# Attention block of a three-stage kernel: where TensorE issues the weighted-value products of a half

## The chip, the cores and the metric

One NeuronCore of a Trainium2 chip runs the whole program. The metric is device time in microseconds (us) of one execution. The engines have these names in the rows: PE is TensorE's matmul and PEld its weight load, DVE is VectorE, ACT is ScalarE, POOL is GpSimd, SP is the engine whose queue issues the DMAs.

## The reference

Three stages follow each other. The change lies in the first, a clustered attention over 2 batches, 8 heads, 768 tokens and 64 values a head:

```
mask = q_assign[:, :, :, None] == k_assign[:, :, None, :]      # nearest centroid of query and of key
scores = scale * np.matmul(q, k.transpose(0, 1, 3, 2))
scores = np.where(mask, scores, -1000000000.0)
scores = scores - np.max(scores, axis=-1, keepdims=True)
attn = np.exp(scores)
attn = attn / (np.sum(attn, axis=-1, keepdims=True) + 1e-09)
return np.matmul(attn, v)
```

Its output, 1536 tokens of 512 values, goes through a feed-forward block with a rational activation (512 to 2048 to 512) and one with a gated SiLU (512 to 1536 to 512).

## The kernel before

The heads are taken in eight pairs (two heads of a batch). The 768 queries of a pair are cut into two halves of 384, a half into three query blocks of 128, and for each query block there is one step per head: six steps a half, twelve a pair, 96 in all (the list `order`, PER = 6). `n` counts the steps.

A step consists of four parts. `scores` computes 128 queries by 768 keys on TensorE into a PSUM tile s_ps, of which there are two: two matmuls at L376 and two more at L380, which add the remainders and the mask. `maximum` (VectorE, L389) reduces the rows. `exponentials` (ScalarE, L397) writes p and the row sums. `transposes` turns p with six TensorE transposes (L435), three into each of two PSUM tiles t_ps, of which there are three, and two copies to SBUF (L440 on ScalarE; the second copy is VectorE's, L438, in the steps of `dve_evac`). The transposes are issued two steps behind the scores (LAG = 2): TensorE's order is scores(n), transposes(n-2), scores(n+1), transposes(n-1).

Once all six steps of a half are transposed, `weighted` multiplies them by the values: six key blocks (kb = 0 to 5) accumulate in the single PSUM bank o_ps, each with one matmul for each of the two heads (L446). The trace shows every such matmul as two records, so a half has 24. `normalised` (VectorE, L454) multiplies o_ps by the reciprocals of the row sums, which came back by DMA (`spread` with its small transpose r_ps at L412, `bring_back`), and `split_x` (GpSimd, L466 and L467) writes the two parts that the next stage reads.

The main loop runs over units of two steps (n0 and n0 + 1). Three units make a half, so n0 % 6 is 0, 2 or 4. The key blocks of a half are put into the list `pv` at the end of the unit with remainder 0; each later unit takes two off at its end. The order on each engine is the order in which the program issues; nothing reorders it.

`background(n, engine)` issues other work along with the steps: the similarities of the next pair's queries and keys with the centroids (`sims`, L305, TensorE), their cluster masks (VectorE), the split of the next pair's queries and keys (GpSimd), and the unpacking of nine early weight blocks (L82 on ScalarE, L91 and L95 on VectorE). After the loop, `tail` issues the products of the last half in two parts between the first matmuls of the next stage (h_ps, L695).

Of the kernel before, what the change touches and what calls it, by code (L numbers as in the profile page):

```python
# [20 lines left out]
def tile_kernel(ctx, tc, q_t, k_t, q_s, k_s, v_l, cent, w_in, w_out, a_co, b_co, w_gate, w_val, w_o2, out):  # L21
# [5 lines left out]
    NB = S // P  # L27
# [96 lines left out]
    n0, n1 = 2 * GROUP1[0], 2 * GROUP1[1]  # L124
# [41 lines left out]
    PER = 2 * HB  # L166
# [45 lines left out]
    def keep_warm(n, to, x=None):  # L212
        for _ in range(n):
            for j in range(HB):
                nc.tensor.transpose(to[:, j, :], ident if x is None else x[:, 0:P], ident)  # L215
# [154 lines left out]
    def scores(b, hp, half, i, e):  # L370
        t = heads[b, 2 * hp + e]
        s_ps = ps_s.tile([P, S], F32, tag="s", name="s_ps")
        q0 = half * HALF + i * P
        qs = slice(q0, q0 + P)
        for lo, hi in CUT:
            nc.tensor.matmul(s_ps[:, lo:hi], t["q1"][:, qs], t["k1"][:, lo:hi], start=True, stop=False)  # L376
        if (b, hp, half, i, e) == order[0]:
            keep_warm(6, fill, oh[0])
        for lo, hi in CUT:
            nc.tensor.matmul(s_ps[:, lo:hi], t["q2"][0:KM, qs], t["k2"][0:KM, lo:hi], start=False, stop=True)  # L380
        if (i, e) == (0, 0):
            st = live["st", b, hp, half] = st_p.tile([P, 3, PER], F32, tag="st", name="st")
            nc.vector.memset(st[:, 2, :], 1e-9)
        live["s", b, hp, half, i, e] = s_ps

    def maximum(b, hp, half, i, e):
        st = live["st", b, hp, half]
        k = e * HB + i
        nc.vector.tensor_reduce(  # L389
            out=st[:, 0, k:k + 1], in_=live["s", b, hp, half, i, e], axis=AX.X, op=ALU.max, negate=True  # L390
        )

    def exponentials(b, hp, half, i, e):
        st = live["st", b, hp, half]
        k = e * HB + i
        p = live["p", b, hp, half, i, e] = p_p.tile([P, S], F32, tag="p", name="p")
        nc.scalar.activation(  # L397
            out=p, in_=live.pop(("s", b, hp, half, i, e)), func=AF.Exp, bias=st[:, 0, k:k + 1],
            accum_out=st[:, 1, k:k + 1],
        )  # L400

    def reciprocals(b, hp, half):
        st = live["st", b, hp, half]
        nc.vector.tensor_reduce(
            out=st[:, 0, :], in_=st[:, 1:3, :].rearrange("p a k -> p k a"), axis=AX.X, op=ALU.add
        )
        nc.vector.reciprocal(out=st[:, 0, :], in_=st[:, 0, :])

    def spread(b, hp, half):
        st = live.pop(("st", b, hp, half))  # L410
        r_ps = t_tile("r_ps")[0:PER, 0, :]
        nc.tensor.transpose(r_ps, st[:, 0, :], ident)  # L412
        rs = rs_p.tile([PER, P], F32, tag="rs", name="rs")
        nc.scalar.copy(out=rs, in_=r_ps)
        rd = tc.dram_tile([2, HALF], F32, name="rd")
        nc.sync.dma_start(out=rd.rearrange("e (i p) -> (e i) p", p=P), in_=rs)
        live["rd", b, hp, half] = rd

    def bring_back(b, hp, half):
        rd = live.pop(("rd", b, hp, half))  # L420
        rb = live["rb", b, hp, half] = rb_p.tile([P, HALF], F32, tag="rb", name="rb")
        for e in range(2):
            nc.sync.dma_start(out=rb[e * D:(e + 1) * D, :], in_=rd[e:e + 1, :].to_broadcast([D, HALF]))

    def transposes(b, hp, half, i, e, on_dve):
        p = live.pop(("p", b, hp, half, i, e))
        if i == 0:
            live["pt", b, hp, half, e] = pt_p.tile([P, NB, HALF], F32, tag="pt", name="pt")
        pt = live["pt", b, hp, half, e]
        qc = slice(i * P, (i + 1) * P)  # L430
        for g in range(2):
            t_ps = t_tile("t_ps")
            for j in range(HB):
                kb = g * HB + j
                nc.tensor.transpose(t_ps[:, j, :], p[:, kb * P:(kb + 1) * P], ident)  # L435
            ks = slice(g * HB, (g + 1) * HB)
            if g == 1 and on_dve:
                nc.vector.tensor_copy(out=pt[:, ks, qc], in_=t_ps)  # L438
            else:
                nc.scalar.copy(out=pt[:, ks, qc], in_=t_ps)  # L440

    def weighted(b, hp, half, kb):
        if kb == 0:
            live["o", b, hp, half] = ps_v.tile([P, HALF], F32, tag="o", name="o_ps")
        for e in range(2):
            nc.tensor.matmul(  # L446
                live["o", b, hp, half][e * D:(e + 1) * D, :], heads[b, 2 * hp + e]["v"][:, kb, :],
                live["pt", b, hp, half, e][:, kb, :], start=(kb == 0), stop=(kb == NB - 1),
                tile_position=(0, e * D),
            )  # L450

    def normalised(b, hp, half):
        x = live["x", b, hp, half] = x_p.tile([P, HALF], F32, tag="x", name="x")
        nc.vector.tensor_tensor(  # L454
            out=x, in0=live.pop(("o", b, hp, half)), in1=live.pop(("rb", b, hp, half)), op=ALU.mult
        )

    def split_x(b, hp, half):
        x = live.pop(("x", b, hp, half))
        done = 0  # L460
        while done < HALF:
            t, o = divmod(b * S + half * HALF + done, T)
            n = min(HALF - done, T - o)
            hi = x_hl[t][:, 0, hp, o:o + n]
            src = x[:, done:done + n]
            nc.gpsimd.tensor_scalar(out=hi, in0=src, scalar1=1.0, scalar2=0.0, op0=ALU.mult, op1=ALU.add)  # L466
            nc.gpsimd.tensor_tensor(out=x_hl[t][:, 1, hp, o:o + n], in0=src, in1=r32(hi), op=ALU.subtract)  # L467
            done += n
# [54 lines left out]
    def q_rows(t, half):  # L523
        nc.scalar.activation(
            out=t["q2"][D:D + 32, cols[half]], in_=t["t3"][32 * half:32 * half + 32, :],
            func=AF.Identity, scale=MASKED, bias=msk[32 * half:32 * half + 32, 1:2],
        )
# [13 lines left out]
    pv = []  # L541
# [48 lines left out]
                    load_qk(b, 2 * hp + 1)  # L590

    LAG = 2
    def next_weighted():
        if pv:
            step = pv.pop(0)
            weighted(*step)
            if step[3] == NB - 1:
                return step[:3]


    for n0 in range(0, len(order) + LAG, 2):
        for n in (n0, n0 + 1):
            if n < len(order):
                scores(*order[n])
                maximum(*order[n])
            if n == 1:
                keep_warm(3, fill)
            if n >= LAG:
                transposes(*order[n - LAG], n % (2 * PER) in dve_evac)
            if n < len(order):  # L610
                exponentials(*order[n])
            if n == 1:
                q_rows(h1, 1)
                for t in (h0, h1):
                    del t["t3"]
            if n % PER == 0 and n:
                reciprocals(*order[n - 1][:3])
            if n % PER == RS and n > PER:
                spread(*order[n - RS - 1][:3])
            elif n == len(order) + 1:  # L620
                spread(*order[-1][:3])
            if n % PER == BB and n > PER:
                bring_back(*order[n - BB - 1][:3])
            for engine in ("dma", "pe", "dve", "pool", "act"):
                background(n, engine)
        finished = next_weighted()
        finished = next_weighted() or finished
        if finished:
            normalised(*finished)
            split_x(*finished)  # L630
        if n >= LAG and (n - LAG) % PER == PER - 1:
            pv.extend([order[n - LAG][:3] + (kb,) for kb in range(NB)])
    bring_back(*order[-1][:3])
# [12 lines left out]
    with ExitStack() as mctx:  # L646
# [292 lines left out]
        for n in range(NS):  # L939
# [20 lines left out]
            if pipe:  # L960
                _, reciprocal, quotient, remainder = pipe.pop()
# [139 lines left out]
        asked = set()  # L1101
        LAG = {"act": 1.7, "dve": 1.7, "pool": 3.5, "dma": 5.5, "set": 0.0}

# [104 lines left out]
        _, reciprocal, quotient, remainder = pipe.pop()  # L1208
        mm, _ = project(*seq[NS - 3])
# [12 lines left out]
        mm, _ = project(*seq[NS - 2])  # L1222
# [199 lines left out]
```

## Time and profile before

| what | us |
|---|---|
| median of three runs | 780.5 (780.27 to 780.78) |
| span of the profiled execution, first to last instruction | 779.4 |
| median less span | 1.1 |
| TensorE matmul busy | 773.3 |
| VectorE, ScalarE, GpSimd busy | 594.4, 510.9, 457.4 |

The profiled execution's own time is recorded as its span; the median of the timed runs stands 1.1 us above it. A busy time is the sum of an engine's instructions without their overlaps. Ends of matmuls are modelled, so a busy TensorE is not TensorE at its peak.

### The profile page before, as it was taken

What the parts mean: (1) busy time and instruction counts of PE and PEld (TensorE: products, weight loads), DVE (VectorE), ACT (ScalarE), POOL (GpSimd) and SP (SyncE); (2) the same over time, 40 slices, a digit from 0 to 9 for tenths busy, and PEclk for the clock granted to TensorE, in tenths of its full rate; (3) what the DMA queues carried; (4) which work ended last, traced back from release to release, by engine and by line L of the source; (5) the groups of instructions that cost most, each with busy time, mean ns of one, the idle gap of its engine ahead of it and who ended that gap; (6) DMA issues with size and microseconds to landing.
All of it is one profiled execution on the core that took longest, in us unless ns stands there. A gap on an engine that the chain in (4) does not pass through costs nothing.

```text
span 779.4 us, 11585 instructions
## 1 busy us (share of the span) xinstructions
PE 773.3 (99%) x4119; PEld 637.7 (82%) x4119; DVE 594.4 (76%) x894; ACT 510.9 (66%) x984; POOL 457.4 (59%) x429
## 2 busy tenths in 40 slices
PE   8999999999999999999999999999999999999998
PEld 7666666666767888888888888999999999999997
DVE  7778787778659999989999999997565655675454
ACT  8777777777776788787777768646645545454331
POOL 6476797678334676767777688764354544534410
PEclk9999999999999999999999999999999999999999
DMA  7266436533322211211211111013222112120013
GB/s 224 76 203 205 153 99 202 178 115 114 98 79 78 81 56 66 70 55 56 81 55 53 56 33 49 27 55 100 90 82 81 55 55 82 55 81 28 1 41 122
DMA packets 27209, 67.94 MB, mean 87 GB/s; under 512 B 4464, under 2 KB 10832, under 8 KB 27152
## 3 DMA queue, kind: packets, MB, share of 16 engines
q1 hardware_dynamic: 27152, 67.21, 26.3%
q8 instruction: 32, 0.52, 0.3%
q14 instruction: 25, 0.20, 0.1%
HBM read 59.48 MB, written 3.19 MB: 80 GB/s over the span
## 4 chain that ended last, share of the span: by engine, by line
PE 98%; DVE 1%; SPq 1%; DMA 0%; ACT 0%; issue 0%; POOL 0%; POOLq 0%
PE c_ps L1012 23%; PE h_ps L695 17%; PE acc L751 17%; PE acc L1069 13%; PE o_ps L446 8%; PE t_ps L435 8%; PE s_ps L376 5%; PE s_ps L380 4%; PE w_ps L215 1%; PE sim L305 1%; SPq L366 1%; DMA k<-t 0%; DVE st L389 0%; PE r_ps L412 0%; PE acc L1368 0%
## 5 line engine op out<-in xcount | busy, mean ns | idle before, releaser
L1012 PE MATMUL c_ps<-r,wb 128*128 128x384 f32 x648 | 125.3, 336 | 0.0
L1012 PEld LDWEIGHTS c_ps<-r,wb 128*128 128x128 f32 x648 | 115.4, 188 | 6.0
L389 DVE TENSOR_REDUCE st<-s_ps 128x1 f32<-128x768 f32 x96 | 91.5, 953 | 31.3 <-PE s_ps L380 30.5
L397 ACT ACTIVATE p<-s_ps,st 128x768 f32<-128x768 f32 x96 | 87.7, 913 | 13.6 <-DVE st L389 13.3
L712 POOL TENSOR_TENSOR tmp<-tmp 128x512 f32<-128x512 f32 x46 | 67.9, 1475 | 48.1 <-ACT tmp L711 47.7
L440 ACT COPY pt<-t_ps 128x384 f32<-128x384 f32 x160 | 70.0, 482 | 37.8 <-PE t_ps L435 37.5
L1020 ACT COPY tmp<-c_ps 128x384 f32<-128x384 f32 x60 | 28.8, 480 | 87.3 <-PE c_ps L1012 87.3
L1091 POOL TENSOR_TENSOR part<-tmp,part 128x512 f32<-128x512 f32 x18 | 23.3, 1297 | 101.0 <-ACT tmp L1090 101.0
L435 PE MATMUL t_ps<-ident,p 128*128 128x128 f32 x576 | 78.7, 272 | 0.0
L446 PE MATMUL o_ps<-pt,v 128*64 128x384 f32 x384 | 72.3, 499 | 0.0
L435 PEld LDWEIGHTS t_ps<-ident,p 128*128 128x128 f32 x576 | 66.8, 141 | 4.7 <-issue 0.6
L735 POOL TENSOR_TENSOR g<-td,tmp 128x512 fp32r<-128x512 f32 x45 | 58.5, 1300 | 18.0 <-DVE td L730 18.0
L751 PE MATMUL acc<-g,r 128*128 128x512 f32 x288 | 69.0, 389 | 0.0
L1023 DVE TENSOR_TENSOR tmp<-tmp,c_ps 128x384 f32<-128x384 f32 x40 | 22.2, 555 | 58.9 <-ACT tmp L1020 45.1
L1012 PE MATMUL c_ps<-r,xw 128*128 128x384 f32 x336 | 65.4, 337 | 0.0
L751 PEld LDWEIGHTS acc<-g,r 128*128 128x128 f32 x288 | 54.0, 188 | 11.2
L1012 PEld LDWEIGHTS c_ps<-r,xw 128*128 128x128 f32 x336 | 60.0, 188 | 3.7
L695 PE MATMUL h_ps<-r 128*128 128x512 f32 x252 | 60.8, 391 | 0.0
L1069 PE MATMUL acc<-wb,g 128*128 128x512 f32 x216 | 59.4, 394 | 0.0
L376 PE MATMUL s_ps<-k,q 128*128 128x512 f32 x192 | 58.4, 385 | 0.2 <-ACT p L397 0.2
L695 PEld LDWEIGHTS h_ps<-r 128*128 128x128 f32 x252 | 47.1, 188 | 11.5 <-issue 1.8
L376 PEld LDWEIGHTS s_ps<-k,q 128*128 128x128 f32 x192 | 28.8, 189 | 31.7 <-ACT pt L440 18.0
(169 smaller groups left out, 1774.3 us busy)
## 6 DMA issues: line engine op xcount, KB each, us to landing
raw<-w_in_dram SPq DMA_DIRECT2D x16, 512.0 KB
raw<-w_out_dram SPq DMA_DIRECT2D x16, 512.0 KB
raw<-w_val_dram SPq DMA_DIRECT2D x12, 512.0 KB
raw<-w_gate_dram SPq DMA_DIRECT2D x12, 512.0 KB
raw<-w_o_dram SPq DMA_DIRECT2D x12, 512.0 KB
xa<-q_t_dram SPq DMA_DIRECT2D x14, 384.0 KB
xa<-k_t_dram SPq DMA_DIRECT2D x14, 384.0 KB
sq<-q_s_dram SPq DMA_DIRECT2D x8, 384.0 KB
```

The source lines that it names most:

```text
L376: nc.tensor.matmul(s_ps[:, lo:hi], t["q1"][:, qs], t["k1"][:, lo:hi], start=True, stop=False)
L389: nc.vector.tensor_reduce(out=st[:, 0, k:k + 1], in_=live["s", b, hp, half, i, e], axis=AX.X, op=ALU.max, negate=True)
L397: nc.scalar.activation(out=p, in_=live.pop(("s", b, hp, half, i, e)), func=AF.Exp, bias=st[:, 0, k:k + 1], accum_out=st[:, 1, k:k + 1],)
L435: nc.tensor.transpose(t_ps[:, j, :], p[:, kb * P:(kb + 1) * P], ident)
L440: nc.scalar.copy(out=pt[:, ks, qc], in_=t_ps)
L446: nc.tensor.matmul(live["o", b, hp, half][e * D:(e + 1) * D, :], heads[b, 2 * hp + e]["v"][:, kb, :], live["pt", b, hp, half, e][:, kb, :] ...
L695: nc.tensor.matmul(h_ps, w[:, wi, cs], x[:, xi, cc, :], start=(n == 0), stop=(n == 3 * NCC - 1))
L712: spread.tensor_tensor(out=tq, in0=tq, in1=tr, op=ALU.add)
L735: eng.tensor_tensor(out=g[:, 1, :], in0=td, in1=tr, op=ALU.mult)
L751: nc.tensor.matmul(acc[c], w[:, wi, cs], g[:, gi, :], start=(first and m == 0), stop=(last and m == 2))
L1012: nc.tensor.matmul(live2[key], set_of[f][:, wi, a, cs], x[xi][:, kc, :], start=(first and n == 0), stop=(n == last), skip_group_check=True,)
L1069: nc.tensor.matmul(acc2[j, c], g[:, gi, c * P:(c + 1) * P], w[:, wi, :], start=(f % 2 == 0 and m == 0), stop=(f % 2 == 1 and m == 2),)
```

## The change

The key blocks of a half are taken off the list in another rhythm. The unit with remainder 2, the first behind the one that filled the list, issues all six; the units with remainders 4 and 0 issue none. `normalised` and `split_x` stay at the end of the unit with remainder 0, which now takes the finished half from the list `done_pv`. The tail is unchanged.

```
     LAG = 2
+    BURST = {2: 6, 4: 0, 0: 0}
+    done_pv = []
     def next_weighted():
-        if pv:
-            step = pv.pop(0)
-            weighted(*step)
-            if step[3] == NB - 1:
-                return step[:3]
+        step = pv.pop(0)
+        weighted(*step)
+        if step[3] == NB - 1:
+            done_pv.append(step[:3])
...
-        finished = next_weighted()
-        finished = next_weighted() or finished
-        if finished:
+        for _ in range(min(BURST[n0 % PER], len(pv))):
+            next_weighted()
+        if n0 % PER == 0 and done_pv:
+            finished = done_pv.pop()
             normalised(*finished)
             split_x(*finished)
```

## Rows read from the trace of the kernel before

**Rows 1.** The page: the span, and the clock granted to TensorE in tenths by slice.

```profile
span 779.4 us, 11585 instructions
...
PEclk9999999999999999999999999999999999999999
```

**Rows 2.** Busy times by stretch: start:end, length, busy by engine (instructions), clock, DMA.

```profile
43.65:56.83 13.18, 13.18 (x88) 9.27 (x89) 10.41 (x18) 10.11 (x26) 12.54 (x16) 1.00 0.55 173
56.83:71.00 14.17, 14.17 (x96) 9.46 (x97) 10.60 (x18) 10.13 (x25) 6.91 (x10) 1.00 0.60 197
```

**Rows 3.** The chain of waits, 140 to 190 us: start, duration, engine, tile, line, records.

```profile
146.27 0.78 PE sim L305 x8
...
157.44 1.44 PE o_ps L446 x8
158.88 0.55 PE s_ps L376 x2
...
160.44 0.35 PE s_ps L376 x2
...
161.80 1.44 PE o_ps L446 x8
...
164.80 0.11 PE r_ps L412
```

**Rows 4.** The chain of waits, 217 to 240 us, the end of the stage.

```profile
220.02 1.44 PE o_ps L446 x8
...
228.97 2.95 PE h_ps L695 x12
231.91 2.09 PE o_ps L446 x12
```

**Rows 5.** TensorE's timeline, 200 to 224 us: scores behind a run of products.

```profile
203.72 0.62 PE L376 MATMUL s_ps<-k,q 128*128 128x512 f32 x2
```

**Rows 6.** ScalarE's timeline, 200 to 214 us; in brackets idle time before it.

```profile
200.70 0.86 ACT L440 COPY pt<-t_ps 128x384 f32<-128x384 f32 x2 [0.71 <-PE t_ps L435]
201.45 0.92 ACT L397 ACTIVATE p<-s_ps,st 128x768 f32<-128x768 f32 x1
...
202.34 0.69 ACT L82 ACTIVATE raw<-raw 128x512 f32<-128x512 f32 x1
202.90 0.87 ACT L440 COPY pt<-t_ps 128x384 f32<-128x384 f32 x2
...
205.78 0.90 ACT L397 ACTIVATE p<-s_ps,st 128x768 f32<-128x768 f32 x1 [0.24 <-DVE st L389]
```

**Rows 7.** VectorE's timeline, 200 to 214 us.

```profile
203.84 0.56 DVE L454 TENSOR_TENSOR x<-o_ps,rb 128x384 f32<-128x384 f32 x1 [0.30 <-PE o_ps L446]
204.73 0.96 DVE L389 TENSOR_REDUCE st<-s_ps 128x1 f32<-128x768 f32 x1 [0.34 <-PE s_ps L380]
205.61 0.55 DVE L438 COPY pt<-t_ps 128x384 f32<-128x384 f32 x1
206.07 0.98 DVE L95 SCALAR_TENSOR_TENSOR c<-raw,c 128x512 uint32<-128x512 uint32 x1
206.98 0.94 DVE L389 TENSOR_REDUCE st<-s_ps 128x1 f32<-128x768 f32 x1
```

**Rows 8.** TensorE's timeline, 19.6 to 29.95 us: steps with no products between.

```profile
20.22 0.59 PE L376 MATMUL s_ps<-k,q 128*128 128x512 f32 x2
...
21.98 0.62 PE L376 MATMUL s_ps<-k,q 128*128 128x512 f32 x2 [0.15 <-ACT p L397]
...
23.62 0.62 PE L376 MATMUL s_ps<-k,q 128*128 128x512 f32 x2
...
28.47 1.51 PE L446 MATMUL o_ps<-pt,v 128*64 128x384 f32 x8
```

**Rows 9.** ScalarE's timeline, the same stretch.

```profile
22.54 0.94 ACT L397 ACTIVATE p<-s_ps,st 128x768 f32<-128x768 f32 x1
```

**Rows 10.** TensorE's timeline, 36 to 45 us: a wait for a DMA.

```profile
37.93 0.58 PE L380 MATMUL s_ps<-k,q 80*128 80x512 f32 x2 [0.71 <-DMA k<-t]
```

## The prediction

> **What bounds the kernel now.** I read the page first, for the engine that fills the span and for its clock: the granted clock of TensorE is full in all 40 slices [rows 1], so nothing here is to be won or lost by the clock unless TensorE falls idle for long. Then I read the busy times by stretch, over a half of the attention stage without similarities and one with [rows 2]. TensorE is busy in every microsecond of both, 13.18 of 13.18 us and 14.17 of 14.17 us, while ScalarE has 10.11 and 10.13 us of work in them, VectorE 10.41 and 10.60 us. So TensorE sets the pace with some 3 us to spare on the other two, and what matters is its own order. The chain of waits gives this order [rows 3]: one step (scores, then six transposes) takes 160.44 to 161.80 = 1.36 us, the eight product records of a unit 1.44 us, and the step behind them 158.88 to 160.44 = 1.56 us. The reader is to see that the run of products costs 0.20 us more than its own 1.44 us, paid by the scores behind it.
>
> Next comes the price of a product inside a run. Eight records take 1.44 us [rows 3], twelve in the tail 2.09 us [rows 4]; so each further record costs (2.09 - 1.44)/4 = 0.163 us and the beginning of a run 1.44 - 8 x 0.163 = 0.14 us. Every entry into the products thus costs 0.14 + 0.20 = **0.34 us** beside the products.
>
> Last I read the other engines' pace where no products stand between the steps. The kernel before has such a stretch: before the first half is transposed there are no products, and from the scores at 21.98 us to the first products at 28.47 us four steps run alone [rows 8]. They take 6.49 us, 1.62 us each, where TensorE needs 1.36. ScalarE explains it: two copies 200.70 to 201.45 and an exponential with its read of the sum 201.45 to 202.34 make 0.75 + 0.89 = **1.64 us** a step [rows 6]. The score tile has two buffers, and scores wait for the exponentials two steps earlier: the exponentials at 22.54 us release the scores at 23.62 us, 1.08 us later [rows 8, 9].
>
> **The change part by part.** *What is removed and moved.* Per half, 24 records stand in one run behind the steps of remainder 2 and 3 instead of three runs of eight. The count of instructions is the same, and the moved ones issue no DMA; no queue but TensorE's has another order. Normalisation and split stay where they were on VectorE and GpSimd. TensorE by itself saves two entries a half, 2 x 0.34 = 0.68 us. The run takes 24 x 0.163 + 0.14 = 4.04 us.
>
> *Waits of the run itself.* The last transposed scores that it reads were copied a unit earlier, and its one accumulator bank must be free of the half before: normalisation (0.56 us [rows 7]) follows the maximum of remainder 1, and the run stands two steps later, at least 2.7 us by 1.36 us a step. I cost this at nothing; if that cover went, up to 0.56 us would be added to each of 15 runs, 8 us.
>
> *What is late next.* Behind the run wait the scores and transposes on TensorE, and for them VectorE's maxima and ScalarE's exponentials and copies. In its 4.04 us ScalarE can do only the backlog that the buffers hold and then idles; afterwards six steps come with no products between them, and ScalarE needs 1.64 us for each against TensorE's 1.36. I lay one half out from the moment the run ends (0), by rows.
> The scores start at 0; VectorE's maximum starts 1.01 us later (203.72 to 204.73) and the exponential 1.05 us after that, so at 2.06 [rows 5 to 7]. ScalarE has only the step's two copies before it (the transposes end at 1.56, the last copy some 0.4 behind them), and from here it goes without a gap: the next three exponentials come at 3.70, 5.34, 6.98. Scores of steps 3 to 6 need those of steps 1 to 4 plus 1.08: 3.14, 4.78, 6.42, 8.06, where TensorE alone would want some 2.7, 4.1, 5.5, 6.9. The last step ends 1.56 us after its start, as from 21.98 + 3 x 1.64 = 26.90 to 28.47 us [rows 8]: the next run starts at 9.62. TensorE alone needs 6 x 1.36 + 0.20 + 0.11 (the reciprocals' transpose [rows 3]) = 8.47. So 1.15 us of stall stand against 0.68 saved. The period becomes 9.62 + 4.04 = 13.66 us against 13.18: **+0.48 us**, in six halves of this kind = +2.88.
>
> The halves with similarities (0.78 us on TensorE [rows 3]) give the others that time. There VectorE copies half the tiles of the first two steps and shifts bits: maximum at 1.01, copy 1.89, shift 2.35, next maximum 3.26 (pitches 0.88, 0.46, 0.91 [rows 7]); so the exponentials stand at 2.06, 4.31, 5.95, 7.59, the last scores at 8.67, the next run at 10.23. The period is 14.27 against 14.17, +0.10, five times = +0.50.
>
> Four places differ. (a) The first half: the scores that waited 0.71 us for the masks' DMA and started their second part at 37.93 us [rows 10] now come behind the run (28.47 + 4.04 + 5.48 = 37.99, where 5.48 is the third scores' 3.14 + 1.56 + 0.78 of similarities), so this wait is used up; maximum and exponential of that step give 7.54, the scores two steps later 8.62, the second run 28.47 + 4.04 + 10.18 = 42.69 instead of 43.65 [rows 2]: -0.96. (b) The last pair has no similarities behind it, but the bit shift and a weight block's ScalarE pass (0.56 us, 202.34 to 202.90 [rows 6]): exponential at 7.59 + 0.56 = 8.15, run at 10.79, 14.83 against 13.18 (it is now like the other halves without similarities): +1.65. (c) The half behind it has such a pass too, behind its first exponential: 13.66 + 0.56 = 14.22 against 13.18: +1.04. (d) From the last run to the next stage, 220.02 to 228.97 = 8.95 us now [rows 4]: then 4.04, the last exponential at 4.31 done at 5.39, and its six transposes and the small one 0.66 to 0.82 + 0.11, some 6.2: 10.24, +1.3.
> Sum: -0.96 + 2.88 + 0.50 + 1.65 + 1.04 + 1.30 = **+6.4 us**. The stages behind it are TensorE back to back and only start later. The profiled execution has 779.4 us of span, 1.1 us below the median of 780.5; I add the sum to either: 785.8 of span, **786.9 us**.
>
> **Bounds.** Below: no stall at all, 15 x 0.68 = -10.2 us, 770.3. The stretch of rows 8 speaks against it, so I stay near that. A pitch of 1.61 instead of 1.64 would take 3 x 0.03 x 14 = 1.3 us off. Above: VectorE does the cluster work of the next pair (pieces of about 0.5 to 1 us) between the maxima; if one piece of 0.46 us delays a stalled step in every half, 14 x 0.46 = 6.4 us more, 793.
>
> **Rivals.**
> *Faster: the entries saved are all that counts* (770.3 if wholly so). ScalarE's 10.11 us fit into 12.5 us [rows 2], so a mean over the half says that it keeps up. For this the buffers would have to hold enough work for the run: two score tiles and three transposed ones give at most about an exponential, two copies and another exponential, 0.89 + 0.75 + 0.89 = 2.5 us, against the 4.04 us of the run. It decides from the point where the stall of a half is below 0.68 us, so below 0.17 us in each of the four stalled steps, a pace of about 1.5 us; rows 8 show 1.62. Chance 0.13.
> The Trainium skill speaks for this rival: "TensorE: Matmul & The Clock Gate", section "Loop structure matters more than you think", wants all pieces of the contraction of an output tile issued back to back, so that TensorE stays at its clock. By that rule the sum would be the -10.2 us or better; in this trace the clock is full throughout already, so what the rule is for has nothing to give here.
> *No difference: the stall and the saving cancel*, at 0.68 us of stall a half instead of 1.15; 780.5. Chance 0.09.
> *Much slower: VectorE or the accumulator's release becomes the bound of each half*, the cover above gone: +6.4 + 8, near 795. The margin of two steps speaks against it. Chance 0.05, in the slower side.
>
> **How the numbers follow.** A measurement of this kernel tells 0.2% from nothing, 1.6 us: 778.9 to 782.1 is the same. My forecast (slower by a stall at ScalarE's pace) has 0.73, with the much slower case 0.78 in all; faster 0.13; same 0.09. The range runs from 780 (the stalls cancelled) to 792.5 (the likeliest plus nearly one piece of VectorE work a half), leaving out about 0.13 to 0.15 below and 0.05 above. I put 786.9.
>
> **What would show it.** Right: o_ps in the chain as runs of 24 records and 4.04 us; scores waiting for ScalarE's exponentials in the third to sixth step behind each run, 0.2 to 0.4 us a time; ScalarE idle for some 3 us in each run; TensorE's busy share in the attention stage down by 1 us a half; the end of the first masks' wait. Wrong: scores following each other at 1.36 us behind the run (then the faster rival), the run waiting for the normalisation, or a granted clock below full.

## The result, and the profile after

The changed kernel takes 792.25 us (median of four runs, 791.17 to 792.78) against 780.38 us before: a ratio of 1.0146, with a 95% interval of 1.0133 to 1.0159. It is slower by 11.9 us. The forecast was slower, 786.9 us with a range of 780.0 to 792.5; the time lies at the upper end of that range.

The page of the kernel after, the lines that answer to [rows 1], and its busy times by stretch, answering to [rows 2]: one half without similarities and one with, each from run to run.

```profile
span 790.7 us, 11573 instructions
...
PEclk9999999999999999999999999999999999999999
```

```profile
42.79:57.57 14.78, 13.45 (x86) 9.46 (x86) 10.85 (x17) 10.18 (x27) 13.78 (x18) 1.00 0.57 185
57.57:71.84 14.27, 14.04 (x94) 9.59 (x93) 9.89 (x19) 9.70 (x23) 5.58 (x9) 1.00 0.50 166
```

The reader is to see that the clock is still full, that ScalarE and VectorE have about the same work as before, and that TensorE, busy in every microsecond before, now stands idle for 1.33 us of one half and 0.23 us of the other. The list of TensorE's waits says for whom (line waiting, line waited for, us in all, times, longest):

```profile
PE s_ps L376 <- ACT p L397: 9.3, 23, 1.4
```

Before, that entry had one wait of 0.2 us. ScalarE's timeline at the run that begins at 42.79 shows how little it has to do there: it ends its work at 44.67 us, 1.9 us into the run, and goes on only when the transposes behind the run come.

```profile
44.48 0.19 ACT L397 ACTIVATION_READ_ACCUMULATOR p<-s_ps,st 128x1 f32 x1
48.14 0.86 ACT L440 COPY pt<-t_ps 128x384 f32<-128x384 f32 x2 [3.46 <-PE t_ps L435]
```

TensorE's timeline shows the runs; their starts give the length of each half.

```profile
42.79 4.09 PE L446 MATMUL o_ps<-pt,v 128*64 128x384 f32 x24
57.57 4.09 PE L446 MATMUL o_ps<-pt,v 128*64 128x384 f32 x24
```

From such starts the whole difference can be laid out by the places that the prediction named:

| place | forecast, us | measured, us | from |
|---|---|---|---|
| (a) first half | -0.96 | -0.79 | second run at 42.79 instead of 43.58 |
| six halves without similarities | +2.88 | +8.31 | 87.39 in all against 6 x 13.18 |
| five halves with similarities | +0.50 | +0.51 | 14.27 (once 14.28) against 14.17 |
| (b) last pair | +1.65 | +1.26 | 14.46 against 13.20 |
| (c) the half behind it | +1.04 | +1.00 | 14.19 against 13.19 |
| (d) last run to the tail's first run | +1.30 | +0.85 | 12.74 against 11.89 |
| sum | +6.41 | +11.14 | the span grew by 11.3 |

One term is wrong by 5.4 us, and the others are right within half a microsecond. The question is what the halves without similarities lose beyond the forecast. TensorE's timeline of one of them, from the end of a run to the next:

```profile
46.81 0.61 PE L376 MATMUL s_ps<-k,q 128*128 128x512 f32 x2
...
48.19 0.60 PE L376 MATMUL s_ps<-k,q 128*128 128x512 f32 x2
...
49.95 0.62 PE L376 MATMUL s_ps<-k,q 128*128 128x512 f32 x2 [0.16 <-ACT p L397]
...
51.59 0.62 PE L376 MATMUL s_ps<-k,q 128*128 128x512 f32 x2
...
54.38 0.62 PE L376 MATMUL s_ps<-k,q 128*128 128x512 f32 x2 [1.16 <-ACT p L397]
...
56.02 0.61 PE L376 MATMUL s_ps<-k,q 128*128 128x512 f32 x2
```

Counted from 46.81, the six steps begin at 0, 1.38, 3.14, 4.78, 7.57 and 9.21 us. The forecast had 3.14, 4.78, 6.42 and 8.06 for the last four: exact for two, then 1.15 us late at the fifth. The exponentials that release it are those of the third step, and the timeline of all engines shows what these waited for:

```profile
49.17 0.96 DVE L389 TENSOR_REDUCE st<-s_ps 128x1 f32<-128x768 f32 x1
...
50.04 1.51 DVE L348 TENSOR_TENSOR sm<-wt,mx 128x384 f32<-128x384 f32 x1
...
51.59 0.77 DVE L354 TENSOR_SCALAR sm<-sm,msk 128x384 f32<-128x384 f32 x1
...
52.30 0.94 DVE L389 TENSOR_REDUCE st<-s_ps 128x1 f32<-128x768 f32 x1
...
53.33 0.90 ACT L397 ACTIVATE p<-s_ps,st 128x768 f32<-128x768 f32 x1 [1.04 <-DVE st L404]
```

Between two maxima on VectorE stand two pieces of the next pair's masks, the comparison at L348 (one_hot) and L354 (mask_values), from 50.04 to 52.36 us. The maximum of the third step comes only at 52.30, and ScalarE stands idle for 1.04 us before its exponentials. (The bracket names L404, a small reduction that ends at 53.31; but the exponentials begin 0.09 us behind the end of the maximum at 53.24, as in [rows 6] and [rows 7], 205.69 to 205.78.) VectorE has no gap from 47.81 to 53.24, so a third piece of the masks, L345 (first_reached, 48.68 to 49.22), lies on the same path. In the six halves the length is the duration of the comparison plus a constant:

| run to run, us | 14.78 | 14.60 | 15.01 | 14.28 | 14.43 | 14.29 |
|---|---|---|---|---|---|---|
| comparison L348, us | 1.51 | 1.31 | 1.71 | 1.00 | 1.14 | 1.02 |
| difference, us | 13.27 | 13.29 | 13.30 | 13.28 | 13.29 | 13.27 |

So in these halves VectorE's masks seem to set the pace. This was the theory with which the experiments began; the rival was ScalarE's pace alone.

### The profile page after: what moved, and what is told of

Its sections match the earlier page's. It is cut to its first block, busy times and chain, and to the rows that moved or that the text cites. A ratio compares the mean times of both kernels' runs of the same rounds, so it can differ in the third digit from the quotient of the medians.

```text
span 790.7 us, 11573 instructions
## 1 busy us (share of the span) xinstructions
PE 774.1 (98%) x4119; PEld 640.0 (81%) x4119; DVE 591.0 (75%) x894; ACT 508.5 (64%) x984; POOL 456.9 (58%) x429
## 4 chain that ended last, share of the span: by engine, by line
PE 89%; DVE 5%; ACT 3%; issue 1%; POOL 1%; ACTq 0%; POOLq 0%
PE c_ps L1014 23%; PE h_ps L697 17%; PE acc L753 17%; PE acc L1071 13%; PE o_ps L446 8%; PE s_ps L376 4%; PE t_ps L435 4%; PE s_ps L380 3%; ACT p L397 3%; DVE st L389 3%; DVE sm L348 1%; PE sim L305 1%; DVE sm L354 1%; PE w_ps L215 1%; ACT pt L440 1%
## 5 line engine op out<-in xcount | busy, mean ns | idle before, releaser
L446 PE MATMUL o_ps<-pt,v 128*64 128x384 f32 x384 | 65.7, 491 | 0.0
```

The lines of the kernel that those rows point to most:

```text
L446: nc.tensor.matmul(live["o", b, hp, half][e * D:(e + 1) * D, :], heads[b, 2 * hp + e]["v"][:, kb, :], live["pt", b, hp, half, e][:, kb, :] ...
```

## The experiments

**e1: the masks inside the run.** The last pieces of the masks are issued one unit earlier, where VectorE waits for the run anyway.

```
+                if k:
+                    steps[3:] = [[weigh, first_reached, one_hot, mask_values], [], []]
```

> The changed kernel with one thing moved: VectorE's last three pieces of the next pair's masks (first_reached, one_hot, mask_values) are issued with the step of remainder 3, whose unit ends in the run, instead of with the two steps behind the run. Theory (the masks' pieces, stretched beside GpSimd, stand between the maxima on VectorE and delay the exponentials in the halves without similarities): the run-to-run distance of these halves falls from 14.3 to 15.0 us to the 13.66 us that the prediction worked out, six halves, about 5.4 us in all: some 786.5 us. Rival (ScalarE's pace alone sets these halves, and VectorE's pieces only fill its waits): the distance stays at 14.3 to 15.0 us, and the time at 792.

Measured: 787.06 us, ratio 1.0081 (1.0066 to 1.0096), 5.2 us less than the changed kernel. TensorE's timeline and VectorE's:

```profile
42.68 4.09 PE L446 MATMUL o_ps<-pt,v 128*64 128x384 f32 x24
56.32 4.09 PE L446 MATMUL o_ps<-pt,v 128*64 128x384 f32 x24
70.60 4.09 PE L446 MATMUL o_ps<-pt,v 128*64 128x384 f32 x24
```

```profile
44.56 0.56 DVE L348 TENSOR_TENSOR sm<-wt,mx 128x384 f32<-128x384 f32 x1
```

The half without similarities takes 56.32 - 42.68 = 13.64 us, where the prediction worked out 13.66; the one with them is unchanged at 14.28. The agreement goes down to the single step: counted from the first scores behind the run, the six begin at 0, 1.38, 3.14, 4.78, 6.42 and 8.07 us, and the layout had 3.14, 4.78, 6.42 and 8.06 for the last four. The theory holds, and the rival falls. Which of the three moved pieces costs how much was not separated. What is left above the kernel before, 6.2 us by the medians, is the forecast's own sum of 6.4.

**e2: twice as many entries.** The kernel before, with one key block behind each step (the call of `next_weighted` moves into the loop over n and the second call goes).

> The kernel before with one key block (four records) behind each step instead of two behind each unit of two steps: twice as many entries into the products, three more a half. Theory (each entry costs TensorE 0.34 us, 0.14 at its beginning and 0.20 at the scores behind it): 15 halves x 3 x 0.34 = 15.3 us more, 795.7 us, and the chain all TensorE. Rival (an entry costs nothing of its own, the 0.34 us being a wait of the unit's end): 780.4 us.

Measured: 794.2 us, ratio 1.0173 (1.0157 to 1.0188). The chain of waits:

```profile
158.89 0.80 PE o_ps L446 x4
159.68 0.55 PE s_ps L376 x2
...
161.24 0.80 PE o_ps L446 x4
```

Four records take 0.80 us, that is 4 x 0.163 + 0.15, and the scores behind them 0.55 instead of 0.35: the entry costs 0.35 us here. A step takes 161.24 - 158.89 = 2.35 us instead of 2.18. The total is 2 us short of the 15.3 expected; TensorE's wait for the masks' DMA [rows 10] is no longer in the list of its waits, which gives 0.7 of it, and the rest was not followed up. The saving that the change was worth on TensorE is thus real.

**e3: two runs of three key blocks.** `BURST = {2: 3, 4: 3, 0: 0}`.

> The changed kernel with the six key blocks as two runs of three, in the units of remainder 2 and 4, and none in that of remainder 0. Theory (four steps without products between them starve: the third waits 0.40 us and the fourth some 0.28 us for the exponentials two steps earlier; one entry saved gives 0.34 us): +0.4 us in the halves without similarities, +0.1 in those with, together some 4 us: 784.5 us. Rival (only the long run hurts, since 2.1 us are covered by ScalarE's backlog of 2.5 us): one entry a half saved and no stall, 15 x 0.34 = 5.1 us less, 775.3 us.

Measured: 782.6 us, ratio 1.0023 (1.0012 to 1.0033). TensorE's timeline:

```profile
43.23 2.16 PE L446 MATMUL o_ps<-pt,v 128*64 128x384 f32 x12
48.23 2.16 PE L446 MATMUL o_ps<-pt,v 128*64 128x384 f32 x12
...
53.46 0.62 PE L376 MATMUL s_ps<-k,q 128*128 128x512 f32 x2 [0.16 <-ACT p L397]
...
56.66 2.16 PE L446 MATMUL o_ps<-pt,v 128*64 128x384 f32 x12
...
70.83 2.16 PE L446 MATMUL o_ps<-pt,v 128*64 128x384 f32 x12
```

The half without similarities takes 13.43 us (+0.25), the one with them 14.17 (no change). The sign is the theory's; the size, 1.7 us, is less than half of the expected 4. Four steps without products lose more than one entry gives, and the scores at 53.46, the third behind a run, are the first that wait for exponentials. The rival fails at its premise too, for ScalarE's work does not reach over a run of 2.09 us. It ends 1.9 us into the run that begins at 43.23, as in the changed kernel, and then waits for the transposes behind the run:

```profile
46.65 0.86 ACT L440 COPY pt<-t_ps 128x384 f32<-128x384 f32 x2 [1.53 <-PE t_ps L435]
```

So a shorter run leaves ScalarE idle for a shorter time, 1.53 us instead of 3.46, but it is the number of steps without anything between them that decides whether TensorE has to wait afterwards: e9, below, has runs of twelve with two steps between, and one such wait, of 0.2 us.

**e4: the products between scores and transposes.** In the kernel before, the unit's products stand ahead of the second step's transposes instead of behind them.

> The kernel before with the two key blocks of a unit issued between the second step's scores and its transposes, instead of behind the transposes. It asks which neighbour pays the 0.34 us of an entry. If the 0.20 us is paid only by scores that follow products (and transposes behind products pay nothing): 45 entries x 0.20 = 9 us less, 771.4 us. If any group behind products pays it: 780.4 us. If the transposes' delay starves ScalarE: above 780.4.

Measured: 792.27 us, ratio 1.0146 (1.0129 to 1.0163). The chain of waits:

```profile
160.41 0.49 PE t_ps L435 x3
160.93 0.35 ACT pt L440
...
161.30 0.48 ACT pt L440
161.79 0.90 ACT p L397 x2
...
162.73 0.62 PE s_ps L376 x2
```

The transposes come 1.44 us later, ScalarE's copies stand ahead of the exponentials in its order, and the next scores wait for those. Elsewhere in that chain six transposes behind products take 0.81 us instead of 0.66, so transposes pay too, though less than scores. So the third of the expected outcomes came: the run asked about the entry and found a stronger cost, that products in front of what ScalarE waits for starve it. How the 11.4 us divide between the two was not worked out.

**e5: another order on GpSimd.** In the changed kernel, k_lo of the first head and q_hi with q_scale of the second change places.

```
-                    3: [lambda: k_lo(*a)], 4: [lambda: q_hi(*c), lambda: q_scale(*c)], ...
+                    3: [lambda: q_hi(*c), lambda: q_scale(*c)], 4: [lambda: k_lo(*a)], ...
```

> The changed kernel with two of GpSimd's steps swapped: the subtraction for the first head's keys (k_lo, L284) is issued one step later and the scaling of the second head's queries (q_hi, q_scale) one step earlier, so that another kind of GpSimd work lies beside the masks' comparison on VectorE (L348). In the changed kernel the run-to-run distance of the six halves without similarities was 13.28 us plus the duration of that comparison each time (1.00 to 1.71 us). Theory (GpSimd's subtraction of two tensors beside it stretches the comparison): it takes 0.56 us, the distance is 13.8 to 13.9 us, 0.7 us less in six halves, some 4.3 us in all: 788 us. Rival (the comparison is slow for another reason, such as its broadcast operands): 1.0 to 1.7 us still, and 792 us.

Measured: 792.33 us (790.67 to 793.64), ratio 1.0148 (1.0132 to 1.0165): as the changed kernel, so the time tells nothing. In its profiled run the comparison took 0.55 to 1.02 us, and the lengths followed it again: 13.94 us where it took 0.55, 13.97 at 0.57, 14.43 at 1.02, a constant of 13.4 us. The link from comparison to length is confirmed; that the swap saves time is not. The theory's condition, a subtraction of two tensors, is refuted: beside the longest comparison lay a scaling of one tensor (L271), and the comparison ended at 51.33, 0.41 us behind that scaling's end at 50.92.

```profile
50.09 0.83 POOL L271 TENSOR_SCALAR q<-xa 128x768 fp32r<-128x768 f32 x1
...
50.31 1.02 DVE L348 TENSOR_TENSOR sm<-wt,mx 128x384 f32<-128x384 f32 x1
```

What the comparison waits for can be read in the changed kernel's own rows, GpSimd's three pieces of one subtraction and VectorE's comparison:

```profile
107.85 0.73 POOL L284 TENSOR_TENSOR k<-xa,k 64x256 fp32r<-64x256 f32 x1
...
108.54 0.73 POOL L284 TENSOR_TENSOR k<-xa,k 64x256 fp32r<-64x256 f32 x1
...
109.23 1.05 POOL L284 TENSOR_TENSOR k<-xa,k 64x256 fp32r<-64x256 f32 x1
...
107.97 1.71 DVE L348 TENSOR_TENSOR sm<-wt,mx 128x384 f32<-128x384 f32 x1
```

The comparison begins 0.12 us into the first piece and ends at 109.68, 0.41 us behind the end of the second (109.27); the third is then the one that takes longer, 1.05 us instead of 0.73. In the half shown above it is the same: the third piece begins at 51.10 and takes 1.04, and the comparison ends at 51.55. In all six halves the comparison ended 0.41 to 0.42 us behind the second piece. And the 77 comparisons in the traces of all eleven kernels fall into two kinds: 65 took 0.57 to 1.78 us, and each ended 0.40 to 0.42 us behind the end of a GpSimd instruction; the other 12 took 0.52 to 0.56 us, with no GpSimd instruction under way when they began or one that ended within 0.12 us. So what makes the comparison long is waiting for GpSimd's instruction to end.

The Trainium skill has such a rule, "SBUF — State Buffer", section "SBUF: two separate sides": VectorE, with two inputs from SBUF, and GpSimd share a pair of ports, which whoever begins first keeps for its whole instruction. The traces agree in that the comparison waits for a GpSimd instruction's end and the next GpSimd instruction is then longer. They differ in that a comparison that began in the first piece was let in only behind the second, and no run here shows the ports themselves.

**e6 and e7: more work for ScalarE.** One copy from PSUM is done twice in each half, in the unit of remainder 0: in e6 added to e1, in e7 to the kernel before.

```
                 nc.scalar.copy(out=pt[:, ks, qc], in_=t_ps)
+                if g == 0 and twice:        # n % PER == 1
+                    nc.scalar.copy(out=pt[:, ks, qc], in_=t_ps)
```

> The kernel of e1 (changed kernel, masks inside the run) with one copy from PSUM done twice on ScalarE in each half, in the unit of remainder 0, four steps behind the run (0.375 us of pitch, 0.48 us of busy time). Theory (ScalarE works without a gap from the end of the run to the last scores, so each microsecond added to it delays the next run): +0.375 us in each of some 14 halves, 5.2 us, 792.3 us. Rival (the latency of scores, maximum and exponential through two score tiles sets the pace of 1.64 us, with slack on ScalarE): within 1 us of e1's 787.1 us.

> The kernel before with the same doubled copy. Both theories: ScalarE has some 3 us to spare in a half, and the copy is hidden: 780.4 us. If ScalarE is already at its limit in that unit: up to 15 x 0.375 = 5.6 us more.

Measured: e6 794.58 us, ratio 1.0179 (1.0165 to 1.0193), 7.5 us above e1; e7 781.22 us, ratio 1.0008 (0.9998 to 1.0017), no difference that can be told. ScalarE's timeline in e6 (L442 is the second copy), and two runs:

```profile
54.17 0.54 ACT L440 COPY pt<-t_ps 128x384 f32<-128x384 f32 x1
54.75 0.48 ACT L442 COPY pt<-t_ps 128x384 f32<-128x384 f32 x1
55.12 0.49 ACT L440 COPY pt<-t_ps 128x384 f32<-128x384 f32 x1
```

```profile
43.94 4.09 PE L448 MATMUL o_ps<-pt,v 128*64 128x384 f32 x24
58.11 4.09 PE L448 MATMUL o_ps<-pt,v 128*64 128x384 f32 x24
```

The half without similarities grows from 13.64 to 14.17 us, 0.53, and the one with them from 14.28 to 14.74, 0.46; some 14 halves and a first run that begins 0.8 us later account for the 7.5. The expectation's 0.375 was the pitch of independent copies; this one, writing the same place, begins 0.58 us behind the first. So behind a run this copy is not hidden, and in the kernel before the same copy costs 1.3 us at most by the interval. The rival, a pace set by latency with slack on ScalarE, falls.

**e8 and e9: the rule turned round.** If TensorE needs something to do in each pair of steps and nothing more, the similarities can be one such gap. e8 is the kernel before with the products behind every even step; the halves whose window holds the similarities take two runs of three.

```
+    GAPS = {2: 2, 4: 2, 6: 2, 8: 3, 10: 3}     # key blocks behind step n % 12
+    LATE = {8: 2, 10: 2, 0: 2}                 # from n = 80 on, without similarities
...
+                for _ in range((LATE if n >= 80 and n % (2 * PER) in LATE else GAPS).get(n % (2 * PER), 0)):
+                    done_pv.append(next_weighted())
```

> The kernel before with the products placed by the theory: behind every second step stands something that TensorE can do without ScalarE, and nothing more. In the halves whose window holds the similarities (0.78 us, behind the step of remainder 0) these serve as one such gap, so the six key blocks go in two runs of three, behind the first and third step of the window; in all other halves three runs of two, behind every second step. Theory (a gap of products or similarities in every two steps covers the 3.14 us from scores to the scores two steps later, and an entry saved is worth 0.34 us): six entries fewer, 6 x 0.34 = 2.0 us less, 778.4 us. Rival (the longer distances of the products starve ScalarE or VectorE there): 780.4 us or more.

Measured: 779.84 us, ratio 0.9988 (0.9979 to 0.9997): 0.7 us less by the medians and 0.9 by the ratio, where 2.0 were expected. The chain of waits shows what was late:

```profile
102.48 0.96 DVE st L389
103.44 1.54 DVE sm L348
...
105.01 0.77 DVE sm L354
...
106.75 1.00 ACT p L397 x2
...
107.80 0.62 PE s_ps L376 x2
```

It is the comparison again: in this order it stands behind the maximum of a step that no products follow. e9 moves the masks' pieces to the even steps.

```
+                if k:
+                    steps[1:] = [[], [largest, reached], [], [weigh, first_reached], [], [one_hot, mask_values]]
```

> The kernel of e8 with the masks' pieces on VectorE moved from one a step to the even steps, those that a run of products follows (two, two and two pieces with the steps of 2, 4 and 6 of a pair; the first piece stays with 0 and the last with 6). In e8 the comparison and its neighbour stood behind the maximum of step 5, which has no run behind it, and the unit behind the step 7 was 0.1 to 0.6 us late in most pairs. Theory (VectorE is late only where its extra work falls between two maxima with no products after the first): these waits go, a pair takes 26.99 to 27.01 us instead of 27.15 to 27.61, together some 2 us less than e8: 778.0 us. Rival (the waits of e8 have another cause, such as the doubled distance of the products): as e8, 779.8 us.

Measured: 779.3 us, ratio 0.9981 (0.9972 to 0.9990). TensorE's timeline, the first run of products of one pair and of the next:

```profile
135.54 2.16 PE L446 MATMUL o_ps<-pt,v 128*64 128x384 f32 x12
...
162.53 2.16 PE L446 MATMUL o_ps<-pt,v 128*64 128x384 f32 x12
```

This pair takes 162.53 - 135.54 = 26.99 us, where the kernel before takes 13.18 + 14.17 = 27.35. Four of the five pairs from 53.84 us on take 26.97 to 27.11 us, where e8 has 26.99 once and 27.15 to 27.61 otherwise, so the waits of e8 are gone there. The fifth takes 27.72: its run of products waited 0.63 us for normalisation, which stood on VectorE behind a comparison of 1.77 us. e9 is faster than both kernels, by 0.2% of the one before. Its gain by the ratio, 1.5 us, is short of the 2.0 us of six entries, its runs spread from 778.2 to 781.3 us, and the times alone do not tell it from e8, whose interval overlaps.

## Why the prediction was right, and which term was too small

The entry's price of 0.34 us held (e2: 0.35), the run took 4.02 us in the chain against 4.04, ScalarE stood idle for 3.46 us at a run, and the pace behind it was 1.64 us: the two steps that only ScalarE set came at 3.14 and 4.78 us, as worked out. The halves with similarities came out at 14.27 us, as forecast. Places (a) to (d) were 0.04 to 0.45 us off; of the 0.17 us of (a), 0.07 come from setting the chain's 43.65 against the timeline's clock, where that run begins at 43.58. The wait for the masks' DMA is gone from TensorE's list.

The step that failed is the layout of a half without similarities, where ScalarE "goes without a gap" and the exponentials stand at 5.34 and 6.98 us. The masks' pieces on VectorE were given no weight in it; they appeared only under the bounds, as one piece of 0.46 us in every half. They cost 0.62 to 1.35 us in six halves, 5.4 us in all. That the time still lies inside the range is partly luck: the upper end was set by a smaller piece in all fourteen halves, 6.4 us, and what came was a larger one in six, nearly the same sum. In the kernel before, VectorE does both pieces while TensorE issues products, and the maximum behind them at 50.38 waits for its scores and not for them:

```profile
47.93 1.51 PE L446 MATMUL o_ps<-pt,v 128*64 128x384 f32 x8
...
48.26 0.83 DVE L348 TENSOR_TENSOR sm<-wt,mx 128x384 f32<-128x384 f32 x1
49.12 0.87 DVE L354 TENSOR_SCALAR sm<-sm,msk 128x384 f32<-128x384 f32 x1
...
50.38 0.96 DVE L389 TENSOR_REDUCE st<-s_ps 128x1 f32<-128x768 f32 x1 [0.38 <-PE s_ps L380]
```

That is why they cost nothing there; without products between the steps they stand between two maxima. The comparison takes 0.55 to 1.25 us in the kernel before and 0.71 to 1.71 in the changed one, by what GpSimd is doing when it begins (e5). e1 took the term away, and the half fell to 13.64 us against the 13.66 of the layout.

Of the rivals, the faster one saw a true saving and missed how little of ScalarE's work the buffers hold: 1.9 us were done in the run, where the prediction estimated at most 2.5, and e3 loses with half the run. The Trainium skill's rule that spoke for it ("TensorE: Matmul & The Clock Gate", section "Loop structure matters more than you think") had nothing to give, as the clock was full in both kernels. Of the much slower rival, one half was true in another form: VectorE became the bound of six halves, by the masks and not by the accumulator's release; in the changed kernel no run of products waited for VectorE.

## What to carry to other kernels

Work on the bound engine that needs no other engine is also cover for the others' work: before gathering it into one run, lay out the order of every engine for the stretch that is left without it, small pieces of side work included, with the durations that they have beside what the other engines do then. With two buffers between TensorE and ScalarE, two steps in a row without such cover were free here, a third was not (e3). Saving entries pays where some other work already gives the cover, as the similarities do in e9.

## What the runs showed of the hardware

The same comparison of 128x384 elements on VectorE took 0.52 to 0.56 us where no GpSimd instruction was in its way and up to 1.78 us otherwise, ending 0.40 to 0.42 us behind the end of a GpSimd instruction, a subtraction or a scaling; the piece of a subtraction that followed took 1.05 instead of 0.73 us. A copy from PSUM on ScalarE that writes where the copy ahead of it wrote began 0.58 us behind it, where independent copies follow each other by 0.37 us. Transposes behind products took 0.81 us for six instead of 0.66, scores 0.90 for four matmuls instead of 0.70.
